# The experts as straight-line code: three groups of 256 tokens for the first, one of 128 for each other, and a general path behind one branch

## The chip, the cores and the metric

The kernel runs on one core of a Trainium2 chip. The metric is the device time of one execution, in microseconds. A run of it is compared with runs of the kernel before on the same chip, and medians are compared.

## The reference

Three layers follow each other. An attention with a decaying state, 4 batches of 768 tokens, 8 heads of 48 features; a feed-forward layer with softplus over all 3072 tokens; and a layer of eight experts that each token enters with its best expert alone, or not at all.

```python
def _attn_ref(q, k, v, f_logit):
    f = 1.0 / (1.0 + np.exp(-f_logit))
    for t in range(S):
        state = f[:, :, t, :, None] * state + np.einsum('bhd,bhe->bhde', k[:, :, t], v[:, :, t])
        y[:, :, t] = np.einsum('bhd,bhde->bhe', q[:, :, t], state)

def _moe_ref(x, w_in, w_out):            # [3072, 384] @ [384, 2048], [2048, 384]
    h = x @ w_in
    g = np.maximum(h, 0.0) + np.log1p(np.exp(-np.abs(h)))
    return g @ w_out

def _moe2_ref(x, w_skip, w_gate, w1, w2): # w1: 8 x [384, 1024], w2: 8 x [1024, 384]
    do_compute = x @ w_skip > 0
    xc = x[do_compute]
    logits = xc @ w_gate
    e_idx = np.argmax(logits, axis=1)
    gate_w = softmax(logits)[np.arange(len(xc)), e_idx]
    for e in range(8):
        mask = e_idx == e
        h = np.maximum(xc[mask] @ w1[e], 0.0)
        y[mask] = gate_w[mask, None] * (h @ w2[e])
    out = x.copy(); out[do_compute] = xc + y
```

How many tokens an expert gets depends on the data, so the kernel learns it while it runs.

## The kernel before

Every product that must be exact is made of three matmuls: each operand is split in a rounded part (`hi`, a 32-bit type that TensorE takes in one pass) and what that lacks (`lo`), and hi x hi, hi x lo and lo x hi are added up. Plain float32 is used where little is computed.

The program runs in 96 steps, eight for each unit of 256 tokens. A step has one eighth of the unit's feed-forward layer: `Ffn.up` (L417: 18 matmuls of 256 columns into `ph`), the softplus on ScalarE, VectorE and GpSimd (L432 to L453), and `Ffn.down` two steps later (L464: 12 matmuls of 394 columns into `acc`). The last columns of `w_out` carry its product with the routing weights, so the routing logits come out with the features. The attention of later tokens (L238 to L387) and the conversion of the weights lie between these steps. `Route` then picks each token's expert, stores the token's row to `x_s` in memory, and writes its number into a table sorted by expert. The last unit's numbers go by a shorter way (`last_route`: `place`, L537, and `set_ids`, L604).

The experts take turns, the one with most tokens first. An expert's weights come in quarters (`w_load`, L641; halves of w1, then of w2), are split by `w_split` (L656: the `hi` cast on ScalarE L665, the `lo` difference L673, on VectorE or GpSimd), and live in slots that are given out and back in the order of the program. A tile of 128 tokens is gathered by its numbers (L681), turned by three transposes (`turn`, L691), and taken through `expert` (L929): `up` (L941) with the tokens as weights and w1 as the moving operand in pieces of 512, 256 and 256 columns, a relu, eight transposes (`flip`, L947) that turn the hidden layer, `down` (L958) with 384 columns, the result `om` (L987) and the scatter of its rows to the output (L988).

The first expert's first tile is prepared beside the layer (`first_ids`). Before the experts one branch asks two flags (L901), and each expert's further tiles stand under branches of their own (`more`, L992, on the count that is loaded into a register). What stands inside a branch is scheduled by itself. Outside, a scheduler orders the instructions of each engine; `pin` keeps those of the experts in the order written. Each engine takes its instructions in that order, and SyncE (SP) issues the loads and stores in its own.

Of the kernel before, what the change touches and what calls it, by code (L numbers as in the profile page):

```python
# [19 lines left out]
P = 128  # L20
UNIT = 256
NEST = 6
FIRST = 0
FILL = (4, 2, 2, 5)
FILL0 = (0, 0, 2, 5)
AHEAD = 4
# [16 lines left out]
def gla_softplus_moe_kernel(  # L43
# [22 lines left out]
    E, _, F2 = w1.shape  # L66
# [15 lines left out]
    mw = ctx.enter_context(tc.tile_pool(name="mw", bufs=1))  # L82
    ps = ctx.enter_context(tc.tile_pool(name="ps", bufs=1, space=PSUM))
    main = ctx.enter_context(ExitStack())
    first = ctx.enter_context(ExitStack())
    att = first.enter_context(tc.tile_pool(name="att", bufs=2, side="right"))
    ffn = main.enter_context(tc.tile_pool(name="ffn", bufs=2))
    wp = main.enter_context(tc.tile_pool(name="wp", bufs=1))

    def psm(name):  # L90
        return ps.tile([P, 512], F32, tag="m", name=name, bufs=4)

# [26 lines left out]
    id0 = const.tile([P, 2], I32, name="id0")  # L119
# [12 lines left out]
    wo_hi = wp.tile([P, NF, XR], F32R, name="wo_hi")  # L132
    wo_lo = wp.tile([P, NF, XR], F32R, name="wo_lo")
# [3 lines left out]
    def setup():  # L137
# [7 lines left out]
        # [s <= t]  # L145
# [16 lines left out]
        ve.memset(hmax, 0.0)  # L162
        for t in [a_all, ut] + v_end:
# [25 lines left out]
    def conv_w(g, j):  # L189
# [3 lines left out]
        sl = (slice(None), slice(None), slice(g * n, (g + 1) * n)) if j == 0 else \  # L193
            (slice(None), slice(2 * g, 2 * g + 2), slice(0, DM))
        hw, lw = (wi_hi[sl], wi_lo[sl]) if j == 0 else (wo_hi[sl], wo_lo[sl])
# [3 lines left out]
        # below the least float32 the value is taken as 0  # L199
# [11 lines left out]
    def route_cols(g, w):  # L211
        """w_out @ [w_skip | w_gate] for two tiles of its rows, so that a token's logits come with its features."""
# [12 lines left out]
        if g % 2:  # L225
# [4 lines left out]
            sl = (slice(None), slice(2 * g - 2, 2 * g + 2), slice(DM, XR))  # L230
            se.copy(wo_hi[sl], src)
            ve.tensor_tensor(wo_lo[sl], src, wo_hi[sl].bitcast(F32), op=ALU.subtract)  # L232

# [15 lines left out]
    def a_pre(c):  # L249
# [4 lines left out]
        # the decay's exponent since the chunk's first token, then from its middle  # L254
# [8 lines left out]
        # a decay beyond the bound is taken step by step  # L263
# [16 lines left out]
    def split_qk(qt, kt):  # L280
        """Both in two exact parts, with q's heads side by side and zeros on the other head's rows."""
# [31 lines left out]
    def a_score(c):  # L313
# [14 lines left out]
        # the heads of a pair sit on different rows of the array: a PSUM bank each  # L328
# [25 lines left out]
        # 32 of the array's columns each: the first features of four heads, or the last of a pair  # L354
# [46 lines left out]
    class Ffn:  # L401
# [7 lines left out]
        def up(self, i):  # L409
            xh, xl = self.x  # L410
            ph = ps.tile([P, 2, UNIT], F32, tag="h", name=f"ph{i}", bufs=2)
            for j in range(2):
                f0 = (2 * i + j) * P
                n = 0
                for kk in range(KD):
                    for w, x in ((wi_hi, xh), (wi_hi, xl), (wi_lo, xh)):
                        te.matmul(ph[:, j, :], lhsT=w[:, kk, f0:f0 + P], rhs=x[:, kk, :],  # L417
# [220 lines left out]
    def w_free(kind, n):  # L638
        slots.append(taken.pop((kind, n)))
# [231 lines left out]
    def redo_unit(b, j):  # L871
# [19 lines left out]
        if final:  # L891
            return
# [218 lines left out]
```

## Time and profile before

| | us |
|---|---|
| median of three runs | 897.87 |
| the runs | 898.48, 897.87, 888.36 |
| span of the profiled execution | 890.6 |
| TensorE busy | 735.6 |
| VectorE busy | 690.5 |
| last matmul of the feed-forward layer ends | 687.05 |
| last matmul of the experts ends | 879.76 |

The profiled execution's time is known by its span, from the first to the last instruction; what lies around it is not shown. TensorE's matmuls overlap, so what one costs in a series is the distance between two starts, and not its duration. The granted clock is the mean share of full speed that TensorE got in a stretch; it has two levels, 1.2 and 2.4 GHz.

### The profile page before, as it was taken

The page shows a single profiled execution, that of the slowest core. Times are in us where ns is not written, and L with a number is a line of the kernel's source. Part 1 is how long each engine was busy: PE and PEld are TensorE (multiplying, and loading weights), DVE is VectorE, ACT ScalarE, POOL GpSimd, SP SyncE. Part 2 cuts the span into 40 slices and gives each one's busy share as a digit, 9 for nine tenths or more (in the row PEclk, how much of TensorE's full clock was granted, in tenths as well). Part 3 has the DMA queues.
Part 4 walks back from the last instruction along what each step waited for, and adds up shares of the span by engine and source line. Part 5 has one row for each costly group of instructions (what it writes and reads, how often), then busy time and mean ns, then how long its engine had stood idle before and what let it go on. Part 6 is the DMA issues. An engine that isn't in the chain of part 4 may idle for free. (4 is left out here: it accounts for less than half of the span.)

```text
span 890.6 us, 15792 instructions
## 1 busy us (share of the span) xinstructions
PE 735.6 (83%) x5857; PEld 674.5 (76%) x5857; DVE 690.5 (78%) x1180; ACT 458.7 (52%) x881; POOL 464.9 (52%) x382
## 2 busy tenths in 40 slices
PE   1676788989989997998989799897997889777665
PEld 1465667979989886998878699897896789666554
DVE  7999998888798779788887978888786733756651
ACT  4555544556556555555556655554654422545430
POOL 7777766763665757375666635454442421334220
PEclk9989869999999999899999899999999899878877
DMA  9553221221111211112121110101511681555400
GB/s 297 162 157 111 82 66 40 77 32 56 42 58 44 63 48 51 47 42 76 42 72 35 50 55 23 47 1 41 210 37 30 214 270 36 169 167 177 158 22 5
DMA packets 44040, 75.97 MB, mean 85 GB/s; under 512 B 5439, under 2 KB 23186, under 8 KB 43920
## 3 DMA queue, kind: packets, MB, share of 16 engines
q1 hardware_dynamic: 41040, 68.66, 24.8%
q0 software_dynamic: 2880, 5.82, 2.2%
q8 instruction: 62, 1.02, 0.5%
q14 instruction: 58, 0.48, 0.2%
HBM read 63.23 MB, written 12.11 MB: 85 GB/s over the span
## 5 line engine op out<-in xcount | busy, mean ns | idle before, releaser
L444 POOL TENSOR_TENSOR w<-w,u 128x512 f32<-128x512 f32 x95 | 129.9, 1368 | 173.9 <-DVE u L437 133.8
L417 PE MATMUL ph<-xh,wi_hi 128*128 128x256 f32 x576 | 169.4, 294 | 22.9 <-DVE u L437 12.1
L417 PE MATMUL ph<-xl,wi_hi 128*128 128x256 f32 x576 | 165.5, 287 | 0.0
L417 PE MATMUL ph<-xh,wi_lo 128*128 128x256 f32 x576 | 164.8, 286 | 0.0
L464 PE MATMUL acc<-wo_hi,gh 128*128 128x394 f32 x384 | 139.0, 363 | 12.1 <-ACT gh L452 10.1
L464 PE MATMUL acc<-wo_hi,gl 128*128 128x394 f32 x384 | 132.7, 360 | 19.5 <-DVE gl L453 19.5
L464 PE MATMUL acc<-wo_lo,gh 128*128 128x394 f32 x384 | 134.6, 351 | 2.2 <-DVE wo_lo L232 2.2
L417 PEld LDWEIGHTS ph<-xh,wi_hi 128*128 128x128 f32 x576 | 113.0, 196 | 28.6 <-issue 11.0
L443 ACT ACTIVATE w<-w 128x512 f32<-128x512 f32 (+1 forms) x97 | 60.7, 626 | 104.6 <-DVE u L436 104.6
L417 PEld LDWEIGHTS ph<-xl,wi_hi 128*128 128x128 f32 x576 | 112.9, 196 | 0.3 <-issue 0.2
L417 PEld LDWEIGHTS ph<-xh,wi_lo 128*128 128x128 f32 x576 | 112.7, 196 | 0.2 <-issue 0.2
L434 DVE TENSOR_SCALAR w<-u 128x512 f32<-128x512 f32 (+1 forms) x97 | 71.7, 739 | 41.3 <-ACT u L433 39.7
L673 DVE TENSOR_TENSOR lo<-raw,hi 128x384 fp32r<-128x384 f32 (+1 forms) x88 | 65.1, 786 | 38.3 <-ACT hi L665 38.2
L464 PEld LDWEIGHTS acc<-wo_hi,gl 128*128 128x128 f32 x384 | 75.0, 196 | 25.4 <-DVE gl L453 24.8
L436 DVE SCALAR_TENSOR_TENSOR u<-w,u 128x512 f32<-128x512 f32 (+1 forms) x97 | 86.7, 894 | 1.7
L464 PEld LDWEIGHTS acc<-wo_hi,gh 128*128 128x128 f32 x384 | 74.3, 194 | 17.5 <-ACT gh L452 13.1
L452 ACT CAST gh<-w 128x512 fp32r<-128x512 f32 (+1 forms) x97 | 59.3, 611 | 47.0 <-POOL w L444 45.8
L453 DVE TENSOR_TENSOR gl<-w,gh 128x512 fp32r<-128x512 f32 (+1 forms) x89 | 65.7, 738 | 20.2 <-ACT gh L452 19.7
L464 PEld LDWEIGHTS acc<-wo_lo,gh 128*128 128x128 f32 x384 | 75.1, 196 | 2.8 <-DVE wo_lo L232 2.6
L432 ACT ACTIVATE u<-ph 128x512 f32<-128x512 f32 (+1 forms) x97 | 56.5, 582 | 23.0 <-PE ph L417 22.8
L437 DVE SCALAR_TENSOR_TENSOR u<-ph,u 128x512 f32<-128x512 f32 (+1 forms) x97 | 65.8, 679 | 2.3
L433 ACT ACTIVATE u<-u 128x512 f32<-128x512 f32 (+1 forms) x97 | 60.9, 628 | 1.3
(211 smaller groups left out, 1740.9 us busy)
## 6 DMA issues: line engine op xcount, KB each, us to landing
raw<-in_moe_w_dram SPq DMA_DIRECT2D x32, 768.0 KB
si<-in_moe_w_in_dram SPq DMA_DIRECT2D x8, 768.0 KB
so<-in_moe_w_out_dram SPq DMA_DIRECT2D x8, 768.0 KB
f<-in_f_logit_dram SPq DMA_DIRECT2D x24, 224.0 KB
q<-in_q_dram SPq DMA_DIRECT2D x24, 224.0 KB
k<-in_k_dram SPq DMA_DIRECT2D x24, 224.0 KB
x_s<-xr SPq DMA_DIRECT2D x24, 192.5 KB
v<-in_v_dram SPq DMA_DIRECT2D x24, 192.0 KB
```

The lines of the kernel that those rows point to most:

```text
L417: te.matmul(ph[:, j, :], lhsT=w[:, kk, f0:f0 + P], rhs=x[:, kk, :], start=(n == 0), stop=(n == 3 * KD - 1))
L432: se.activation(u[:, c], ph[:, c], AF.Abs)
L433: se.activation(u[:, c], u[:, c], AF.Exp, scale=-1.0)
L434: ve.tensor_scalar(w[:, c], u[:, c], 1.0, None, op0=ALU.add)
L436: ve.scalar_tensor_tensor(u[:, c], w[:, c], 1.0, u[:, c], op0=ALU.subtract, op1=ALU.subtract)
L437: ve.scalar_tensor_tensor(u[:, c], ph[:, c], 0.0, u[:, c], op0=ALU.max, op1=ALU.subtract)
L443: se.activation(w[:, c], w[:, c], AF.Ln)
L444: (ve if i in self.fine else ge).tensor_tensor(w[:, c], w[:, c], u[:, c], op=ALU.add)
L452: se.copy(flat(gh)[:, c], w[:, c])
L453: (ge if i < self.pool_steps else ve).tensor_tensor(flat(gl)[:, c], w[:, c], flat(gh)[:, c].bitcast(F32), op=ALU.subtract)
L464: te.matmul(self.acc[t][:, 0:XR], lhsT=g[:, j, t * P:(t + 1) * P], rhs=w[:, f, :], start=(f == 0 and n == 0), stop=(f == NF - 1 and n == 2))
L673: pin((ge if i == 0 and n % 4 != 1 else ve).tensor_tensor(lo[:, i], t[:, i], hi[:, i].bitcast(F32), op=ALU.subtract))
```

## The change

The experts become one straight line of code without branches. The first expert gets `UNITS0` = 3 groups of 256 tokens, each other expert one tile of 128, whatever the counts are. Two flags (a decay that is too strong; now also any expert over its places, `flag_counts`) are asked once, at the end: where one is set, a general path does the experts again. It is in the program but not part of the main line.

A group or tile is a `Tiles`. Its `up` has w1 as the weights and the tokens as the moving operand, 256 columns wide for a group and 128 for a tile, so the hidden layer comes out with its features on the partitions, and the transposes of `flip` are gone. `act` makes both parts straight from PSUM. A step of `down` follows the next step's `up`. The splits are two pieces of 768 a quarter, ScalarE then VectorE (GpSimd has none); `feed` puts up to three of them behind each step of a tile, and issues loads when slots are free. The layer's weights are tiles per step, so that memory for the experts' weights comes free step by step. On the host w1 and w2 are laid out so that a quarter is one run of 6 KB per partition. The layer's own matmuls and activations stay.

```diff
-NEST = 6
-FIRST = 0
-FILL = (4, 2, 2, 5)
-FILL0 = (0, 0, 2, 5)
-AHEAD = 4
+UNITS0 = 3
+TILES0 = UNITS0 * UNIT // P
+PIECES = 2
+FILL = (0, 0, 2, 3) + (3,) * 64
...
-    wi_hi = wp.tile([P, KD, DFF], F32R, name="wi_hi")
-    wi_lo = wp.tile([P, KD, DFF], F32R, name="wi_lo")
...
+        for g in range(STEPS):
+            wi_hi[g] = wp.tile([P, KD, 2 * P], F32R, name=f"wi_hi{g}")
+            wi_lo[g] = wp.tile([P, KD, 2 * P], F32R, name=f"wi_lo{g}")
...
+    def w_piece(n, i):
+        m = KD * F2 // 2 // PIECES
+        t, hi, lo = (w.rearrange("p a c -> p (a c)")[:, i * m:(i + 1) * m] for w in (raw[n], w_hi[n], w_lo[n]))
+        pin(se.copy(hi, t))
+        pin(ve.tensor_tensor(lo, t, hi.bitcast(F32), op=ALU.subtract))
+        if i == PIECES - 1:
+            slots.append(taken[n].pop(0))
+    def feed(n):
+        while True:
+            while wanted and len(slots) >= (1 if wanted[0][0] == "load" else 2):
+                what, q = wanted.pop(0)
+                if what == "load":
+                    w_load(q)
+                else:
+                    pieces.extend(w_split(q))
+            if n <= 0 or not pieces:
+                return
+            w_piece(*pieces.pop(0))
+            n -= 1
+    class Tiles:
...
+        def up(self, i):
+            xh, xl = self.x
+            ph = self.ph[i] = ps.tile([P, self.per, self.n * P], F32, tag="h", name=f"phm{i}", bufs=2)
+            for j in range(self.per):
+                f = i * self.per + j
+                g, c = 4 * self.e + f // 4, slice(f % 4 * P, (f % 4 + 1) * P)
+                n = 0
+                for kk in range(KD):
+                    for w, x in ((w_hi[g], xh), (w_hi[g], xl), (w_lo[g], xh)):
+                        pin(te.matmul(ph[:, j, :], lhsT=w[:, kk, c], rhs=x[:, kk, :], start=(n == 0),
+                                      stop=(n == 3 * KD - 1)))
+                        n += 1
+        def act(self, i):
+            ph = self.ph.pop(i).rearrange("p a b -> p (a b)")
+            gh, gl = (pools["mo"].tile([P, self.per, self.n * P], F32R, tag=nm, name=nm) for nm in ("hh", "hl"))
+            flat = lambda a: a.rearrange("p a b -> p (a b)")
+            pin(se.activation(flat(gh), ph, AF.Relu))
+            pin(ve.scalar_tensor_tensor(flat(gl), ph, 0.0, flat(gh).bitcast(F32), op0=ALU.max, op1=ALU.subtract))
...
-    bad, redo = flags()
-    with tc.If(redo > 0, preferred_fallthrough_block=False):
...
+    wanted += [("load", n) for n in range(4, 12)] + [("split", n) for n in range(4, 8)] + [("load", n) for n in range(12, 16)]
+    for e in range(2, E):
+        wanted += [("split", n) for n in range(4 * e, 4 * e + 4)]
+        if e + 2 < E:
+            wanted += [("load", n) for n in range(4 * e + 8, 4 * e + 12)]
+    feed(0)
+    pinned.append(True)
+    route = last_route()
+    next(route)
...
+    for at in range(len(seq) + 1):
+        if at < len(seq):
+            w, i = seq[at]
+            while pieces and pieces[0][0] <= 4 * w.e + (1 if i == 0 else 3):
+                w_piece(*pieces.pop(0))
+            w.up(i)
+            w.act(i)
...
+        feed(FILL[at])
+        if at >= 1:
+            w, i = seq[at - 1]
+            w.down(i)
...
+    some = nc.values_load(flag[0:1, 1:2], min_val=0, max_val=1)
...
+    with tc.If(some > 0, preferred_fallthrough_block=False), ExitStack() as gen:
```

Three places where instructions stand otherwise than before. First TensorE at the end of the feed-forward layer (`acc` are the layer's sums, `phm` the experts' hidden layer, `first` the first tokens), before:

```order
L464 MATMUL acc_7405<-wo_hi,gl 128x394
L568 MATMUL pids<-ident,rows 128x96
L903 UNCONDITIONAL_BRANCH x2
L523 MATMUL pr<-roh,before 128x16
L524 MATMUL pr<-cnt_last,ones 128x16
L554 MATMUL pplace<-pcol,prow 128x192
L608 MATMUL pcnt<-cnt_all,ones 128x8
L554 MATMUL pplace<-pcol,prow 128x192
L691 MATMUL pxg<-ident,xg_7573 128x128 x3
L902 UNCONDITIONAL_BRANCH
L941 MATMUL phm_11991<-hi_7246,first_7749 128x512
```

and now:

```order
L736 MATMUL phm_7858<-first_7581,w_7270 128x256
L736 MATMUL phm_7858<-first_7581,w_7269 128x256
L736 MATMUL phm_7858<-first_7582,w_7269 128x256
L481 MATMUL acc_7422<-wo_hi_130,gh 128x394
L481 MATMUL acc_7422<-wo_lo_131,gh 128x394
L481 MATMUL acc_7423<-wo_hi_130,gh 128x394
L481 MATMUL acc_7423<-wo_lo_131,gh 128x394
L736 MATMUL phm_7858<-first_7581,w_7270 128x256
```

The experts' matmuls, behind a branch before (whose rows between are not run unless a flag is set), now stand between the layer's last ones. The first 18 of them, the first group's first step of `up`, come ahead of the routing of the last unit.

Second SyncE's queue, around the last unit's stores (`out_dram` and `x_s`). Now, in this order, nine loads stand ahead of these stores, eight of them like the last one shown:

```order
L666 DMA w_7789<-in_moe_w_dram 128x1536
L666 DMA w_7803<-in_moe_w_dram 128x1536
L666 DMA w_7813<-in_moe_w_dram 128x1536
L502 DMA out_dram<-xr 128x384 x2
L528 DMA x_s<-xr 128x385 x2
L666 DMA w_8002<-in_moe_w_dram 128x1536
```

Before, two loads stood there and the other 26 behind the branch. All but the first of the nine now wait for TensorE to have done with a piece of the layer's weights.

Third VectorE, through one expert of one tile (`w` are weights in split, `hl` the lower part of the hidden layer, `xl` that of the next tile's turned tokens, `om` the result):

```order
L745 SCALAR_TENSOR_TENSOR hl<-phm_9102,hh 128x512
L677 TENSOR_TENSOR w_9010<-w_8847,w_9009 128x768 x2
L677 TENSOR_TENSOR w_9074<-w_8849,w_9073 128x768 x2
L745 SCALAR_TENSOR_TENSOR hl<-phm_9174,hh 128x512
L677 TENSOR_TENSOR w_9144<-w_8851,w_9143 128x768 x2
L677 TENSOR_TENSOR w_9146<-w_8853,w_9145 128x768
L764 SCALAR_TENSOR_TENSOR om<-pom,xg 128x384
L411 TENSOR_TENSOR xl<-pxg,xh 128x384
L677 TENSOR_TENSOR w_9146<-w_8853,w_9145 128x768
```

All eight pieces of the next expert's weights lie on VectorE now, four and four around the tile's own two evacuations, in place of 11 of 14 smaller ones, the other three on GpSimd.

## Rows read from the trace of the kernel before

**Rows 1.** The page: the span, and busy time of each engine, share, count.

```profile
span 890.6 us, 15792 instructions
...
PE 735.6 (83%) x5857; PEld 674.5 (76%) x5857; DVE 690.5 (78%) x1180; ACT 458.7 (52%) x881; POOL 464.9 (52%) x382
```

**Rows 2.** Busy time of each engine by stretch, then granted clock, DMA share, GB/s.

```profile
0.00:20.00 20.00, 2.28 (x16) 2.04 (x18) 16.46 (x30) 8.88 (x13) 14.19 (x29) 1.00 0.94 293
...
640.00:660.00 20.00, 19.79 (x128) 19.27 (x127) 16.42 (x35) 10.29 (x19) 8.10 (x7) 0.91 0.29 105
...
740.00:760.00 20.00, 19.57 (x126) 18.18 (x125) 6.97 (x15) 6.10 (x13) 4.66 (x5) 1.00 0.14 41
...
820.00:840.00 20.00, 11.77 (x60) 9.80 (x59) 11.87 (x18) 8.19 (x19) 5.62 (x6) 0.83 0.55 178
```

**Rows 3.** Timeline of L987, the tiles' results: start, us, instruction, wait before it.

```profile
758.54 0.62 DVE L987 SCALAR_TENSOR_TENSOR om<-pom,xg 128x384 f32<-128x384 f32 x1 [0.69 <-PE pom L958]
773.01 0.61 DVE L987 SCALAR_TENSOR_TENSOR om<-pom,xg 128x384 f32<-128x384 f32 x1
...
879.80 0.62 DVE L987 SCALAR_TENSOR_TENSOR om<-pom,xg 128x384 f32<-128x384 f32 x1 [1.06 <-PE pom L958]
```

**Rows 4.** Timeline of TensorE: the layer's end, the experts' start and end.

```profile
686.53 0.52 PE L464 MATMUL acc<-wo_hi,gl 128*128 128x394 f32 x2
690.99 0.76 PE L941 MATMUL phm<-hi,first 128*128 128x512 f32 x1 [3.94 <-DVE rmx L512]
...
879.42 0.34 PE L958 MATMUL pom<-hi,hl 128*128 128x384 f32 x1
```

**Rows 5.** Waits from 765 to 880 us: who, for whom, us, times, longest.

```profile
PE phm L941 <- issue: 27.6, 6, 5.7
```

**Rows 6.** Timeline of TensorE: series at full clock, first and last starts.

```profile
153.20 0.84 PE L224 MATMUL pw<-wt,wsg 128*32 128x128 f32 x6
...
300.63 0.28 PE L417 MATMUL ph<-xh,wi_hi 128*128 128x256 f32 x1
...
301.91 0.28 PE L417 MATMUL ph<-xh,wi_lo 128*128 128x256 f32 x1
...
762.18 0.60 PE L947 MATMUL pht<-ident,hr 128*128 128x128 f32 x4
...
875.75 0.33 PE L958 MATMUL pom<-lo,hh 128*128 128x384 f32 x1
...
877.31 0.34 PE L958 MATMUL pom<-lo,hh 128*128 128x384 f32 x1
```

**Rows 7.** Single lines, durations in ns (min/median/max); last: a group, us and mean.

```profile
L365 PEld LDWEIGHTS py<-a_sb,v x14: 107/110/112, 302.1 to 302.6; 128*32 128x32 f32 x14
L365 PE MATMUL py<-a_sb,v x14: 270/273/298, 302.1 to 302.7; 128*32 128x128 f32 x14
...
L376 PEld LDWEIGHTS pu<-v,kn x62: 119/123/126, 206.6 to 279.1; 128*48 128x48 f32 x62
...
L417 PEld LDWEIGHTS ph<-xh,wi_hi 128*128 128x128 f32 x576 | 113.0, 196 | 28.6 <-issue 11.0
```

**Rows 8.** Timelines of GpSimd (first gather by the full numbers) and SyncE (weight loads).

```profile
701.45 1.02 POOL L681 DMA_INDIRECT xg<-x_s,idg  x1 [1.88 <-DVE tp L612]
...
704.57 126.13 SPq L648 DMA_DIRECT2D raw<-in_moe_w_dram  x24
```

**Rows 9.** VectorE and ScalarE: one split in the timeline, then groups by shape.

```profile
831.85 0.68 DVE L673 TENSOR_TENSOR lo<-raw,hi 128x512 fp32r<-128x512 f32 x1
...
L204 ACT CAST wi_hi<-tw 128x768 fp32r<-128x768 f32 x8 | 6.7, 832 | 16.8 <-DVE tw L203 16.8
L951 DVE TENSOR_TENSOR hl<-pht,hh 128x512 fp32r<-128x512 f32 x13 | 9.0, 690 | 4.1 <-ACT hh L950 4.1
L987 DVE SCALAR_TENSOR_TENSOR om<-pom,xg 128x384 f32<-128x384 f32 x13 | 8.0, 612 | 4.5 <-PE pom L958 4.5
L393 DVE TENSOR_TENSOR xgl<-pxg,xgh 128x384 fp32r<-128x384 f32 x12 | 6.6, 550 | 2.9 <-ACT xgh L392 2.8
```

More of the change, by code (lines that the diff above doesn't have):

```diff
@@ L806, in last_route @@
         yield
+    flag = const.tile([1, 2], I32, name="flag")
     def flags():
@@ L822, in flags, with flag_counts @@
                                 op1=ALU.max)
-        return [nc.values_load(flag[0:1, i:i + 1], min_val=0, max_val=1) for i in range(2)]
+    def flag_counts():
+        t = last.pool.tile([P, E], F32, tag="tq", name="tq", bufs=1)
+        ve.tensor_tensor(t, cnt_all, caps, op=ALU.is_gt)
+        ve.tensor_reduce(over, t, axis=AX.X, op=ALU.max)
+        ve.tensor_tensor(flag[:, 1:2], flag[:, 1:2], over[0:1, :], op=ALU.max)
     def scan_head(b, p, j):
@@ L879, in redo_unit @@
         f = Ffn(xs)
-        final = isinstance(b, int) and (b + 1) * S == NT and (j + 1) * UNIT == S
-        f.acc = last.acc if final else [psm(f"acr{t}") for t in range(CPU)]
+        f.acc = [psm(f"acr{t}") for t in range(CPU)]
         for i in range(STEPS):
@@ L899, in redo_unit @@
             r.scatter(t)
-    bad, redo = flags()
-    with tc.If(redo > 0, preferred_fallthrough_block=False):
-        with tc.If(bad > 0):
+    flags()
+    main.close()
+    mo = pools["mo"] = rest.enter_context(tc.tile_pool(name="mo", bufs=2, reuse_waits="tile"))
+    slots += [("mo", f"w{i}") for i in range(16)]
+    wanted += [("load", n) for n in range(4, 12)] + [("split", n) for n in range(4, 8)] + [("load", n) for n in range(12, 16)]
[3 more added lines that the diff above has]
+            wanted += [("load", n) for n in range(4 * e + 8, 4 * e + 12)]
@@ new lines, in gla_softplus_moe_kernel @@
+    pinned.clear()
+    some = nc.values_load(flag[0:1, 1:2], min_val=0, max_val=1)
+    rest.close()
+    general = ctx.enter_context(ExitStack())
+    ffn = general.enter_context(tc.tile_pool(name="gffn", bufs=2))
+    with tc.If(some > 0, preferred_fallthrough_block=False), ExitStack() as gen:
+        bad = nc.values_load(flag[0:1, 0:1], min_val=0, max_val=1)
+        with tc.If(bad > 0), ExitStack() as again:
+            mw, att, wp = (again.enter_context(tc.tile_pool(name=f"g{nm}", bufs=1)) for nm in ("mw", "att", "wp"))
+            wsg = att.tile([P, KD, 32], F32, name="gwsg")
+            ve.memset(wsg, 0.0)
+            load_wsg()
+            ffn_weights()
+            for g in range(STEPS):
+                load_w(g)
+                for j in range(2):
+                    conv_w(g, j)
@@ L1063 @@
+                    w = Tiles(e, [c[:, 1:2]], ("acc0",), [mo.tile([P, KD, P], F32R, tag=f"gx{i}", name="gx") for i in range(2)])
+                    w.fetch([c[:, 0:1]], "mo")
+                    w.turn()
+                    for i in range(w.steps):
+                        w.up(i)
+                        w.act(i)
+                        w.down(i)
+                    w.out()
 _INS = ["q", "k", "v", "f_logit", "moe_w_in", "moe_w_out", "moe2_w_skip", "moe2_w_gate", "moe2_w1", "moe2_w2"]
```

378 lines of the change are left out of this document (155 added, 223 removed).

## The prediction

> **What bounds the kernel now.** I read the page's busy times first [rows 1]. TensorE is the busiest engine with 735.6 us of a span of 890.6, but that is a mean over stages, so the next view is the busy time by stretch [rows 2]. Beside the feed-forward layer (640 to 660 us) TensorE is busy 19.79 of 20 us: nothing but fewer matmuls would shorten that stage, and the change leaves its matmuls alone. In a stretch of the late experts (820 to 840) it is busy 11.77 of 20 us at a mean granted clock of 0.83: part of the time it ran at the lower of its two levels (1.2 and 2.4 GHz). The change is about this stage.
>
> The timeline of the line that finishes a tile of the experts dates them [rows 3]. There are 13 such rows. The sixth tile ends at 758.54 and the seventh at 773.01, and after it six more come by 879.80, (879.80 - 773.01) / 6 = 17.8 us each. So the first expert took six tiles (641 to 768 tokens) and each other expert one (at most 128). From the last matmul of the feed-forward layer to the first of the experts TensorE idles 3.94 us [rows 4]: from the end of that last matmul (687.05) to that of the last of the experts (879.76) the stage takes 192.7 us. The waits between 765 and 880 us say what the late experts wait for: TensorE stood 27.6 us in six waits with "issue" as the releaser, which no semaphore explains [rows 5]. They stand where one expert's code ends and the next one's begins, around the branches of `more`. That is 27.6 / 6 = 4.6 us of each 17.8.
>
> **The change, part by part.**
>
> *The path taken.* Three groups of 256 hold 768 tokens and seven tiles 128 each. Rows 3 say that this input fits. The other condition of the flag, 256 tokens of the first expert before the last unit, also holds: at least 641, less at most the 256 of that unit, leaves 385. The general path is skipped.
>
> *Branches and flags.* Seven conditional pieces go, and with them the 4.6 us per expert. The one left comes after the last tile, where the kernel before has one too: from the last matmul's end (879.76) to the end of the span lie 10.8 us [rows 4], and I keep them.
>
> *TensorE's work.* All prices are intervals between starts at full clock [rows 6]. A 256-column matmul of the same type: 300.63 to 301.91 over 11 steps, 0.116 us. A 384-column one: 875.75 to 877.31 over 9 steps, 0.173 us. A transpose: four in 0.60, 0.15 us.
> - A group of 256 tokens: 72 matmuls of 256 columns up, 8.35 us, and 48 of 384 columns down, 8.30 us; 16.65, three times: 50.0 us. The 8 transposes of the hidden layer per tile are gone, because w1 is now the weight and the hidden layer comes out as it is needed.
> - One of the other experts: 72 matmuls of 128 columns up and 24 of 384 down (4.15 us). No row has this type at 128 columns. From below it is bounded by its columns, half of 0.116: 0.058 us. From above by plain float32, whose 128-column matmul appears as two records: six in 0.84 us, and one lasts 0.273 [rows 7], so starts are (0.84 - 0.273) / 5 = 0.113 apart, which makes 0.226 us a matmul. Between them lies the weight load. Loads take 0.110 us for 32 columns, 0.123 for 48 and 0.196 for 128 [rows 7], 0.90 ns a column, so 128 columns occupy 0.115 us, and a new one is needed for each matmul. That is nearest to the 256-column row, so I take 0.116: half the columns at no gain. 72 x 0.116 + 4.15 = 12.5 us, seven times: 87.5 us.
> - The Trainium skill (TensorE: Matmul & The Clock Gate, section on LDWEIGHTS) speaks against this part as well: a load takes columns / 1.2 GHz, 107 ns for 128 columns, whatever the matmul behind it. By that rule the 504 matmuls would take 54 us and not 58.5, and the forecast would be 850; the slope of rows 7 agrees with it to a tenth.
> - Turning gathered rows: 33 transposes, 5.0 us.
> - The first group's first 18 matmuls (2.1 us) now stand between the last ones of the layer, where TensorE waits for its activations and then the 3.94 us: hidden.
>
> Sum: 50.0 + 87.5 + 5.0 - 2.1 = 140.4 us.
>
> *New waits.* (a) The second group needs the token numbers with the last unit in them. They were ready at 701.45, when GpSimd began its gathers [rows 8], 14.4 us after the layer; the rest of the first group fills 16.65 - 2.1 = 14.5 us, then two gathers of 1.02 us each must be issued and land. I take 3 us; 0 if the numbers come sooner now, 6 if not. (b) The last step of the last tile waits for ScalarE and VectorE, some 1.3 us. (c) Splits stand in program order with the tiles' own evacuations. A split that waits for its weights holds ScalarE and VectorE, behind it the evacuation of the running step, and behind that TensorE's `down`. I take 5 us over seven experts, between 0 and the price of rival 3. Together 9.3.
>
> *What is taken as free, and its cover.* Splitting: eight pieces of 768 per expert, all on VectorE now (GpSimd did some before). A 512-wide one takes 0.68 us alone [rows 9], so 768 some 1.02. With two evacuations of 0.69, one of 0.55 and one of 0.61 that is 10.7 us per expert, under TensorE's 12.5 + 0.45; ScalarE's eight casts are 8 x 0.832 = 6.7. This cover is 2.2 us thin: if TensorE gets faster, VectorE is the bound. Weights: the nine loads ahead of the last unit's stores on SyncE's queue wait for pieces of the layer's weights to come free, and the stores wait for the layer's last matmul anyway, as those loads do; they cost nothing and land beside the layer. 19 more quarters remain for 150 us. Before, 24 took 126.13 us from the first issue to the last [rows 8], 5.3 us each; at that rate 19 take 100. At the rate of the start (293 GB/s, rows 2) one takes 2.7.
>
> *The total.* 140.4 + 9.3 = 149.7 us in place of 192.7, so 43 less: a span of 848. The span before is 890.6, and the page gives no time around it; the runs' median is 897.87, 7.3 above, and the lowest, 888.36, is below it. I carry the 7.3 over: **855 us**.
>
> **Rivals.**
> 1. *128 columns are taken at float32's price* (slower than before). At 0.226 us the 504 matmuls cost 504 x 0.110 = 55 us more: 910 us, 1.4% over the median. It decides from 0.116 + 43 / 504 = 0.20 us a matmul on. For: nowhere does the kernel before give this type fewer than 256 columns; its attention pads q with zeros to reach 256. Against: every matmul of this type is one record in the trace and plain float32 two.
> 2. *128 columns cost what they are.* At 0.058 us TensorE needs 8.8 us per expert, and VectorE's 10.7 is the bound: 7 x (12.95 - 10.7) = 16 us less, 839. For: weight loads overlap matmuls, and rows 7 have a fixed part that they may share. Against: the slope of rows 7. The Trainium skill (same page, section on the back-to-back gap) has 81 ns for pairs of a load and a 128-column matmul, which would end here too, since VectorE would still be the bound; no run here shows it.
> 3. *The gaps stay in another form.* Splits arrive late, TensorE stands and its clock falls as in rows 2. At a clock of 0.83 the 7 x 12.95 = 91 us of the seven experts become 110, 19 more, and 2 us of standing per expert make 14 where (c) has 5: together 28 more, 883. For: each expert's weights go through load, ScalarE and VectorE just one expert ahead, and loads 16 to 31 can only be issued once the first expert's slots are free. Against: 5.3 us a quarter would suffice, and in 740 to 760, where the first expert's tiles follow each other without a break, the clock was 1.00.
> 4. *The general path runs after all*: 13 tiles again, each with its 12.5 us at least: over 1,000 us. Rows 3 speak against it.
>
> **Numbers.** Forecast 0.55; its own range is 847 (no waits (a) and (c)) to 872 (wait (a) at 6, 2 us per expert at (c), and 5 us for a layer that the scheduler ordered anew). Rival 2 has 0.13, rival 3 0.12, rival 1 0.15, rival 4 0.05. Rivals 1 and 4 make the 2 in 10 left out, so the range is 836 to 891: from rival 2 without wait (a) to rival 3 with wait (a) at 6 and those 5 us. A measurement tells 2% from no change, 18 us: under 880 is faster, over 916 slower. Forecast, rival 2 and a third of rival 3 give 0.72; the rest of rival 3 and most of rival 1 give 0.21 within; rival 4 and the upper end of rival 1 give 0.07.
>
> **What would show it.** In the profile after: no "issue" waits between experts; 13 results written by seven tiles and three pairs; TensorE's starts in the 128-column `up` 0.116 us apart (0.058 and 0.226 for rivals 2 and 1); finished late experts some 13 to 14 us apart in place of 17.8; a clock near 1.00 from 690 us on; no more than a few us of TensorE waiting for VectorE's or ScalarE's splits; weights landing before 687 us. It is wrong if the layer itself ends later than 687 by more than 5 us, since I take it as untouched, if the splits hold TensorE for more than 2 us per expert, or if the branch at the end costs more than the 10.8 us kept.

## The result, and the profile after

The changed kernel takes **871.02 us** in the median of 4 runs (868.43 to 871.37), the kernel before 897.61 of 4 (888.36 to 898.48): a ratio of 0.973, 95% interval 0.968 to 0.977. That is faster, by 26.6 us where the forecast had 43. In a second session the ratio was 0.969 (0.964 to 0.974).

The profiled execution took 871.06 us for a span of 869.4, so 1.7 us lie around a span. The page of the kernel after, as in [rows 1]:

```profile
span 869.4 us, 15749 instructions
...
PE 747.2 (86%) x6119; PEld 702.1 (81%) x6119; DVE 669.0 (77%) x1121; ACT 443.9 (51%) x806; POOL 423.1 (49%) x350
```

TensorE is busy 11.6 us longer and the span is 21.2 shorter: the change removed standing time and added matmul time. The stretches show where, in the columns of [rows 2] (span, then PE, PEld, DVE, ACT, POOL busy, granted clock, DMA share, GB/s):

```profile
680.00:700.00 20.00, 15.46 (x90) 14.68 (x89) 9.19 (x25) 7.07 (x16) 4.54 (x4) 0.83 0.80 326
...
760.00:780.00 20.00, 19.21 (x116) 19.14 (x116) 8.79 (x13) 6.04 (x9) 2.46 (x3) 0.74 0.33 108
780.00:800.00 20.00, 20.00 (x161) 19.93 (x161) 12.40 (x17) 9.11 (x14) 2.37 (x3) 1.00 0.50 189
```

From 780 us on TensorE hardly stands (20.00 of 20 us) and runs at its full 2.4 GHz. Two stretches do not look like that: 680 to 700, with TensorE at 15.46, a clock of 0.83 and 326 GB/s of transfers beside it, and 760 to 780, nearly full but at 0.74.

The results of the experts in the timeline of VectorE answer to [rows 3] ("x2" is a group's pair):

```profile
727.67 1.14 DVE L764 SCALAR_TENSOR_TENSOR om<-pom,xg 128x384 f32<-128x384 f32 x2
744.76 0.61 DVE L764 SCALAR_TENSOR_TENSOR om<-pom,xg 128x384 f32<-128x384 f32 x1
745.62 0.62 DVE L764 SCALAR_TENSOR_TENSOR om<-pom,xg 128x384 f32<-128x384 f32 x1 [0.24 <-PE pom L757]
771.97 1.14 DVE L764 SCALAR_TENSOR_TENSOR om<-pom,xg 128x384 f32<-128x384 f32 x2
786.28 0.61 DVE L764 SCALAR_TENSOR_TENSOR om<-pom,xg 128x384 f32<-128x384 f32 x1
798.85 0.61 DVE L764 SCALAR_TENSOR_TENSOR om<-pom,xg 128x384 f32<-128x384 f32 x1
...
850.61 0.61 DVE L764 SCALAR_TENSOR_TENSOR om<-pom,xg 128x384 f32<-128x384 f32 x1
856.99 0.62 DVE L764 SCALAR_TENSOR_TENSOR om<-pom,xg 128x384 f32<-128x384 f32 x1 [2.91 <-PE pom L757]
```

Thirteen results in three pairs and seven singles; the late experts come 12.5 to 13.1 us apart in place of 17.8. The third pair comes 27 us after the second, though a group has 16.65 us of matmuls.

TensorE's timeline at the first tokens, the layer's end, at the second group's tokens, in the middle of a late expert and at the last matmul answers to [rows 4, 6] (start, us, instruction, wait before it):

```profile
688.29 0.90 PE L724 MATMUL pxg<-ident,xg 128*128 128x128 f32 x3 [4.15 <-DMA xg<-x_s,id]
...
700.09 0.52 PE L481 MATMUL acc<-wo_hi,gl 128*128 128x394 f32 x2
702.63 0.39 PE L540 MATMUL pr<-roh,before 128*128 128x16 f32 x2 [2.02 <-DVE roh L530]
...
719.97 0.38 PE L736 MATMUL phm<-xh,w 128*128 128x256 f32 x1 [0.89 <-ACT xh L410]
721.40 0.38 PE L736 MATMUL phm<-xl,w 128*128 128x256 f32 x1 [1.05 <-DVE xl L411]
...
790.77 0.27 PE L736 MATMUL phm<-xl,w 128*128 128x128 f32 x1
...
794.57 0.28 PE L736 MATMUL phm<-xh,w 128*128 128x128 f32 x1
...
856.61 0.34 PE L757 MATMUL pom<-w,hl 128*128 128x384 f32 x1
```

The 128-column matmul starts every (794.57 - 790.77) / 34 = 0.112 us: the forecast's 0.116, and no rival's 0.058 or 0.226. The Trainium skill (TensorE: Matmul & The Clock Gate, section on LDWEIGHTS) has the columns divided by 1.2 GHz for such a load, an estimate of 107 ns, and that lies as near. But the layer ends at 700.6, not 687.05, and its transposes of the first tokens stood 4.15 us for a gather.

The issues of SyncE (SPq) and the gathers of GpSimd beside that answer to [rows 8]. The first row is the first store of the output, which dates the execution:

```profile
171.50 1.07 SPq L502 DMA_DIRECT2D out_dram<-xr  x2
...
678.13 22.83 SPq L666 DMA_DIRECT2D w<-in_moe_w_dram  x9
```

The same store in the kernel before:

```profile
165.87 1.05 SPq L485 DMA_DIRECT2D out_dram<-xr  x2
```

The gathers:

```profile
681.34 1.05 POOL L699 DMA_INDIRECT xg<-x_s,id  x1 [4.29 <-DVE id L641]
...
711.27 1.01 POOL L699 DMA_INDIRECT xg<-x_s,idg  x1 [25.07 <-DVE over L896]
```

The nine weight loads did not lie beside the layer: they stood behind the table's rows on SyncE's queue, and eight of them went out together from 678.13 to 682.8, three us before the gather of the first tokens. The ninth waited for the layer's end.

The ledger, forecast against trace, from these rows: the first unit's output is stored at 171.50 us where it was at 165.87 (+5.6); from there to the layer's end 529.1 us where it was 521.2 (+7.9); from there to the last matmul's end 156.3 where 149.7 were forecast (+6.6); the tail 12.45 for 10.8 (+1.6). Together 21.7, of the 21.8 between the spans 869.4 and 847.6. The experiments take them one by one.

### The profile page after: what moved, and what is told of

The parts are those of the page before. It is cut to its first block, busy times and chain, and to the rows that moved or that the text cites. A ratio compares the mean times of both kernels' runs of the same rounds, so it can differ in the third digit from the quotient of the medians.

```text
span 869.4 us, 15749 instructions
## 1 busy us (share of the span) xinstructions
PE 747.2 (86%) x6119; PEld 702.1 (81%) x6119; DVE 669.0 (77%) x1121; ACT 443.9 (51%) x806; POOL 423.1 (49%) x350
## 5 line engine op out<-in xcount | busy, mean ns | idle before, releaser
L434 PE MATMUL ph<-xh,wi_hi 128*128 128x256 f32 x576 | 172.4, 300 | 23.5 <-DVE u L454 13.6
L434 PE MATMUL ph<-xl,wi_hi 128*128 128x256 f32 x576 | 168.1, 292 | 0.0
L434 PE MATMUL ph<-xh,wi_lo 128*128 128x256 f32 x576 | 167.8, 291 | 0.0
L481 PE MATMUL acc<-wo_hi,gh 128*128 128x394 f32 x384 | 139.7, 365 | 10.4 <-ACT gh L469 8.6
L434 PEld LDWEIGHTS ph<-xh,wi_hi 128*128 128x128 f32 x576 | 115.6, 201 | 29.4 <-issue 12.8
L434 PEld LDWEIGHTS ph<-xl,wi_hi 128*128 128x128 f32 x576 | 115.5, 201 | 0.3 <-issue 0.2
L434 PEld LDWEIGHTS ph<-xh,wi_lo 128*128 128x128 f32 x576 | 115.3, 200 | 0.2 <-issue 0.2
L451 DVE TENSOR_SCALAR w<-u 128x512 f32<-128x512 f32 (+1 forms) x97 | 66.7, 688 | 42.9 <-ACT u L450 42.8
L481 PEld LDWEIGHTS acc<-wo_hi,gl 128*128 128x128 f32 x384 | 75.1, 196 | 20.5 <-DVE gl L470 19.3
L470 DVE TENSOR_TENSOR gl<-w,gh 128x512 fp32r<-128x512 f32 (+1 forms) x89 | 63.9, 718 | 23.3 <-ACT gh L469 22.9
L736 PE MATMUL phm<-xh,w 128*128 128x128 f32 (+1 forms) x384 | 71.4, 284 | 1.9 <-ACT xh L410 1.7
L745 DVE SCALAR_TENSOR_TENSOR hl<-phm,hh 128x512 fp32r<-128x512 f32 x26 | 18.0, 691 | 64.0 <-ACT hh L744 62.7
```

Of the source, the lines that this page charges most:

```text
L434: te.matmul(ph[:, j, :], lhsT=w[i][:, kk, j * P:(j + 1) * P], rhs=x[:, kk, :], start=(n == 0), stop=(n == 3 * KD - 1))
L451: ve.tensor_scalar(w[:, c], u[:, c], 1.0, None, op0=ALU.add)
L470: (ge if i < self.pool_steps else ve).tensor_tensor(flat(gl)[:, c], w[:, c], flat(gh)[:, c].bitcast(F32), op=ALU.subtract)
L481: te.matmul(self.acc[t][:, 0:XR], lhsT=g[:, j, t * P:(t + 1) * P], rhs=w[f // 4][:, f % 4, :], start=(f == 0 and n == 0), stop=(f == NF - ...
L736: pin(te.matmul(ph[:, j, :], lhsT=w[:, kk, c], rhs=x[:, kk, :], start=(n == 0), stop=(n == 3 * KD - 1)))
L745: pin(ve.scalar_tensor_tensor(flat(gl), ph, 0.0, flat(gh).bitcast(F32), op0=ALU.max, op1=ALU.subtract))
```

## The experiments

The first four ran together on one chip, the next four on one, the last by itself, each time with runs of the kernel before (medians 896.57, 899.53 and 896.91 us).

**again.** No edit: the changed kernel and a second trace.

> The changed kernel once more, with a second trace. In the first trace the output rows of the first unit are stored at 171.50 us, in the kernel before at 165.87, though nothing of the change stands so early in the program. If the 5.6 us belong to the change (its order of loads or its pools), the store comes at about 171.5 again and the layer ends at about 700. If they belong to the one execution, the store can come anywhere between 165 and 172, the distance from it to the layer's end stays at 529, and the kernel's times spread by as much. The gather of the first tokens keeps TensorE waiting 4.5 us in either case, and 760 to 780 us shows a clock near 0.74 again if the half clock at the second expert is the program's.

870.81 us (865.48 to 872.34, 6 runs). The store came at 172.26. In nine traces of the changed kernel and of its variants below, whose programs are alike up to there, it came at 165.9, 166.1, 166.1, 167.7, 168.2, 169.8, 170.0, 171.5 and 172.3. So the 5.6 us belong to the execution and not to the change. The kernel before has them too: its profile has the store at 165.87, nobranch, the same program up to there, at 171.74. What decides it in the first 160 us stays open; the granted clock there differs from trace to trace. The distance to the layer's end was 529.2 again, and 760 to 780 us had a clock of 0.74 again. The half clock is the program's. The distance is so only in part: in the four other traces that keep the nine loads as they are it was 526.4 to 531.3.

**hold.** The first of the nine loads waits for the gather:

```diff
-        sy.dma_start(out=raw[n].rearrange("p a c -> p (a c)"), in_=src)
+        ins = sy.dma_start(out=raw[n].rearrange("p a c -> p (a c)"), in_=src)
+        if n == 4:
+            tc.add_manual_dep(ins.ins, firsts.got.ins.name,
+                              mybir.DependencyInfo(mybir.DependencyClass.Sync, mybir.DependencyReason.DATA))
```

`firsts.got` is the second of the two gathers.

> The first of the nine weight loads that are issued at 678 us waits until the first tokens' gather has landed; the others stand behind it. Theory, collision: the gather took 3.1 to 6.9 us to land because 326 GB/s of weight loads ran beside it. Then the wait of TensorE for the tokens (4.15 + 0.39 us) falls below 1 us, the half clock after it (688 to 693) goes, and the distance from the first unit's output store to the layer's end falls from 529 to about 522: 5 to 8 us less in all. Rival, the gather itself: two gathers issued 0.4 us later than the one before take that long anyway. Then the wait stays above 4 us, the distance at 529, and the loads land 5 us later: no change, or up to 5 us more.

866.22 us (861.74 to 868.60), 4.6 less than again and a little under the 5 to 8 expected, and the two ranges overlap; ratio to the kernel before 0.965 (0.961 to 0.970). The first gather, TensorE at the tokens and at the layer's end:

```profile
673.32 1.05 POOL L702 DMA_INDIRECT xg<-x_s,id  x1 [4.51 <-DVE id L641]
...
677.88 0.55 PE L727 MATMUL pxg<-ident,xg 128*128 128x128 f32 x3 [0.78 <-DMA xg<-x_s,id]
...
687.08 0.52 PE L481 MATMUL acc<-wo_hi,gl 128*128 128x394 f32 x2
```

The gathers, two of them as in the changed kernel, landed in 3.2 us (median) in place of 6.9, and TensorE stood 1.0 us for them in place of 4.5. The collision is shown, and the rival falls. Its price is read from the gather's issue to the layer's end: 14.3 us here and in both and flip, which hold the loads too, 19.3 in the changed kernel, 18.6 to 19.6 in all six traces without. That is 5.0 us. The distance from the store to the layer's end, 521.7 here, promises 7.4, but the other 2.4 lie ahead of the gather, where executions differ anyway (507.4 us from the store to the gather here, 507.4 to 512.0 in the nine traces).

And the stage behind the layer grew from 156.3 to 160.1: TensorE stood 2.4 us for the second group's tokens, a wait that the changed kernel doesn't have, and 740 to 760 us had a clock of 0.82. The gather of those tokens began 5.2 us after their numbers were ready:

```profile
697.18 0.26 DVE L630 TENSOR_SCALAR idg<-ids 128x192 int32<-128x192 int32 x1
...
702.59 1.01 POOL L702 DMA_INDIRECT xg<-x_s,idg  x1 [24.26 <-DVE w L680]
```

The trace's record of transfers says what it waited for: the last unit's rows (`x_s`), which it reads. Their stores were issued from 689.67 on, on the queue of the nine loads and behind them, and moved from 697.7 to 701.4, 1.2 us before the gather; in both they moved until 702.0, and the gather began at 703.24. So the held loads no longer meet the first gather, but they delay the second.

**turn.** The second expert's tokens are turned one step of TensorE earlier:

```diff
-if at < len(seq) and turned < len(work) and turned <= now + 1 and seq[at][1] == seq[at][0].steps - (2 if now >= UNITS0 else 1):
+if at < len(seq) and turned < len(work) and turned <= now + 1 and seq[at][1] == seq[at][0].steps - (2 if now >= UNITS0 - 1 else 1):
```

> The second expert's tokens are turned one step sooner (a step of 4.2 us of TensorE), between the third group's last two steps, so that their split is not asked for right behind the turn. Theory, gap: the waits of 0.83 and 1.03 us at 759 and 761 make the clock fall to half from 762 to 771, with 128-column matmuls 0.21 us apart in place of 0.112. Then both waits go, the clock of that stretch is 1.00, and 5 to 7 us are gained. Rival, the half clock has another cause (the stretch of 18.1 busy us in 740 to 760): the waits go, the clock stays near 0.74, and 2 us at most are gained.

864.64 us (856.44 to 865.75), 6.2 less than again; ratio 0.962 (0.957 to 0.967). First the changed kernel at that place, TensorE with the two engines that it waits for:

```profile
757.57 2.70 DVE L677 TENSOR_TENSOR w<-w,w 128x768 fp32r<-128x768 f32 x3
...
759.44 0.33 PE L736 MATMUL phm<-xh,w 128*128 128x128 f32 x1 [0.83 <-ACT xh L410]
760.79 0.33 PE L736 MATMUL phm<-xl,w 128*128 128x128 f32 x1 [1.03 <-DVE xl L411]
```

Three pieces of a split stand on VectorE ahead of the tokens' own split; TensorE asks for it at once and waits twice, and from 761.8 on its matmuls start 0.21 us apart. The stretch of 760 to 780 with the turn moved, then the layer's last matmuls and the experts' last one:

```profile
760.00:780.00 20.00, 20.00 (x161) 19.93 (x161) 13.06 (x18) 9.13 (x14) 3.46 (x3) 1.00 0.47 152
```

```profile
700.59 0.52 PE L481 MATMUL acc<-wo_hi,gl 128*128 128x394 f32 x2
...
850.01 0.34 PE L757 MATMUL pom<-w,hl 128*128 128x384 f32 x1
```

Both waits are gone, and so is the half clock. The stage takes 149.2 us, 7.1 less, where the forecast had 149.7: this gap, with the clock that fell behind it, was the excess. The length of the waits alone doesn't say whether the clock falls: the second group's tokens wait for the same reason in the changed kernel (0.89 and 1.05 us, at 719.97 and 721.40), and the granted clock of 720 to 740 us is 1.00. What makes the difference no run shows.

**half.** Up projection of the first three late experts with 64 tokens, of the last four with 64 of each 128 hidden units.

```diff
-                        pin(te.matmul(ph[:, j, :], lhsT=w[:, kk, c], rhs=x[:, kk, :], start=(n == 0),
+                        pin(te.matmul(ph[0:self.nf, j, :], lhsT=w[:, kk, c], rhs=x[:, kk, 0:self.n * self.nt], start=(n == 0),
```

`nt` is 64 for the first three, `nf` (and the width of `c`) 64 for the last four; both are 128 elsewhere.

> In the up projection of the second to fourth expert in the order of work, only 64 of 128 tokens are multiplied; in that of the last four all tokens, but only 64 of 128 hidden units of each block (the rest of the computation is left out). Theory, the weights' load: 128 columns of 32-bit weights set the 0.112 us from start to start. Then the first three stay at 0.112, and the last four fall by about 64 columns at 0.90 ns, to 0.05 to 0.07. Rival, the moving columns: the first three fall to 0.056, the last four stay at 0.112. Second rival, a fixed price of an instruction: both stay at 0.112. Where matmuls get faster, VectorE's 10.7 us an expert is the next bound, so the outputs of the last four would come 10.5 to 11 us apart in place of 12.5 to 13.1 by the theory.

TensorE's timeline, first and last start of a series of 36 of either kind, at full clock:

```profile
805.18 0.28 PE L738 MATMUL phm<-xh,w 128*128 128x64 f32 x1
...
809.09 0.28 PE L738 MATMUL phm<-xh,w 128*128 128x64 f32 x1
...
815.85 0.30 PE L738 MATMUL phm<-xh,w 128*64 128x128 f32 x1
...
818.04 0.22 PE L738 MATMUL phm<-xh,w 128*64 128x128 f32 x1
```

Half the tokens: (809.09 - 805.18) / 35 = 0.112 us, nothing gained. Half the weights' columns: 0.063 us. So the load of the weights is the price of this matmul, and its moving columns are free up to 128. Of the last four experts' results the first three came 10.2 us apart, a little under the expected 10.5 to 11. The run's one time, 866.82 us, says little, since the clock stayed low from 760 to 803.

**both.** hold and turn in one kernel.

> The held loads and the sooner turn together. If the two losses are separate, their gains add: hold came out 4.6 us below the changed kernel (866.2 against 870.8) and turn 6.2 us (864.6), so about 860 (858 to 862). If one half clock only takes the other's place (in hold, 740 to 760 us had a clock of 0.82), no more than the better of the two: 863 to 865.

861.08 us (854.66 to 867.84), ratio 0.958 (0.951 to 0.964): near the sum, and the rival's 863 lies inside the spread. The trace has both cures: 522.4 us from store to layer's end, and a clock of 1.00 from 720 to 840.

**flip.** both, and the up projection of the late experts with the tokens as weights; the down products come a step later:

```diff
+            for kk in range(KD):
+                for x, w in ((xh, w_hi[g]), (xh, w_lo[g]), (xl, w_hi[g])):
+                    pin(te.matmul(ph, lhsT=x[:, kk, :], rhs=w[:, kk, :],
...
+            pin(se.activation(self.hr[i], ph, AF.Relu))
...
+            for j in range(self.per):
+                pin(te.transpose(pt[:, j * P:(j + 1) * P], hr[:, j * P:(j + 1) * P], ident))
...
+            pin(se.copy(flat(gh), pt))
+            pin(ve.tensor_tensor(flat(gl), pt, flat(gh).bitcast(F32), op=ALU.subtract))
...
+        feed(FILL[at] + (at < len(seq) and flip(seq[at][0])))
```

The last line gives four pieces of a split to each step of a late expert in place of three, which spreads its eight evenly; the gathered rows have six buffers in place of eight.

> Both, and for the seven late experts the up projection with the 128 tokens as weights and w1's 512 columns moving: 18 matmuls in place of 72, then ReLU, eight transposes of 128 columns back, and the split; the down products come one step later. Theory, the weights' load set the price of the up projection: 512 moving columns at the 0.18 us of 394 columns take 0.23, so 18 x 0.23 + 11 transposes x 0.15 + 24 x 0.173 = 10.0 us of TensorE in place of 12.6, and VectorE's 8 x 0.954 + 2 x 0.69 + 0.56 + 0.61 = 10.2 bounds: outputs 10.2 to 10.8 us apart, 7 x 2.2 = 15 us less than both, so 842 to 848. Rival, the longer chain (ReLU, transposes, split, each on another engine) makes TensorE wait in every step: 11.5 to 12.6 apart, 853 to 862.

**838.93 us** (835.72 to 843.09), ratio 0.934 (0.929 to 0.940): the fastest here, 22.1 us below both and below the 842 to 848 expected; the stage behind the layer takes 130.9 us, both's 152.0. The late experts' results, and a stretch of theirs:

```profile
783.45 0.61 DVE L789 SCALAR_TENSOR_TENSOR om<-pom,xg 128x384 f32<-128x384 f32 x1
...
812.19 0.61 DVE L789 SCALAR_TENSOR_TENSOR om<-pom,xg 128x384 f32<-128x384 f32 x1
818.59 0.62 DVE L789 SCALAR_TENSOR_TENSOR om<-pom,xg 128x384 f32<-128x384 f32 x1 [0.67 <-PE pom L782]
```

```profile
780.00:800.00 20.00, 20.00 (x112) 18.12 (x111) 19.52 (x25) 17.65 (x28) 2.00 (x2) 1.00 0.74 278
```

Three distances of 9.58 us each, with TensorE, VectorE and ScalarE all close to full. The two before them were 11.8 and 11.7; in the mean from the third group to the fifth late expert it is 10.4, within the 10.2 to 10.8 expected of VectorE's bound. The last distance, 6.40, is not an expert's price: the fifth result stood 2.9 us on VectorE behind the splits, the sixth came right behind its last matmul, and the last matmuls of the two end 9.2 us apart. TensorE never waits in this stretch, so the longer chain costs nothing there. What the even feeding of the splits adds to the turned operand was not separated.

**small.** The first expert's second and third group as four tiles of 128, the turn a step earlier from the second tile on:

```diff
-    for u in range(1, UNITS0):
-        work.append(Tiles(0, [ids[:, 0, 2 * u + t:2 * u + t + 1] for t in range(2)], ("acc0", "acc1"),
-                          firsts.x if u == 2 else two(2)))
+    for t in range(2, TILES0):
+        work.append(Tiles(0, [ids[:, 0, t:t + 1]], (f"acc{t % 2}",), two(1)))
```

> The changed kernel, with the first expert's second and third group as four tiles of 128 in place of two groups of 256. If a tile of 128 costs what the late experts cost (12.6 us) and a group 16.65, the kernel takes 4 x 12.6 - 2 x 16.65 = 17 us longer, 886 to 891, so that two groups carry more than half of the change's 27 us. If other waits bound that stretch (the routing's numbers, the weights' splits), less than 10 us: 872 to 880.

875.12 us (872.16 to 880.90); its ratio of 0.976 (0.969 to 0.984) can't be told from again's 0.969 (0.964 to 0.974). The trace says why it is so little:

```profile
735.48 0.62 DVE L764 SCALAR_TENSOR_TENSOR om<-pom,xg 128x384 f32<-128x384 f32 x1 [0.85 <-PE pom L757]
748.07 0.62 DVE L764 SCALAR_TENSOR_TENSOR om<-pom,xg 128x384 f32<-128x384 f32 x1 [0.85 <-PE pom L757]
```

The tiles cost 12.6 us each, as expected, and with the turn's place changed the clock does not fall at the second expert (760 to 780 us: 1.00). Its stage of 165.7 us is 9.4 over the changed kernel's 156.3, and 16.5 over turn's 149.2, which like it has no half clock there: that is the expected 17. The 17 were right and the verdict of 872 to 880 came out all the same, because this kernel also undoes a loss that it was not meant to touch.

**notail.** No general path and no branch to it.

```diff
-    some = nc.values_load(flag[0:1, 1:2], min_val=0, max_val=1)
-    with tc.If(some > 0, preferred_fallthrough_block=False), ExitStack() as gen:
...
```

> The changed kernel without the general path at its end and without the branch to it (left out: what is done for inputs that need it; these do not). The changed kernel's trace ends 12.45 us after the last matmul. If the branch is on the path that sets the end, as its engines meet for it after the last store is issued, 2 to 6 us of them go. If the last store's landing and the program's end set it, 11 to 12.5 stay.

One run, 865.86 us, with a span of 864.1 us. The last matmul in its timeline:

```profile
857.02 0.34 PE L757 MATMUL pom<-w,hl 128*128 128x384 f32 x1
```

From the last matmul's end to the span's 6.7 us in place of 12.45: the branch that is never taken costs 5.7 us, with the load of its flag, on the path that sets the end.

**nobranch.** The kernel before, without the late experts' branches:

```diff
-        more(e, n, second, *((xt2, xg["third"]) if e == 0 else ()))
+        if e == 0:
+            more(e, n, second, xt2, xg["third"])
```

> The kernel before, without the seven late experts' branches to further tiles (line 1034 for e > 0, with the gather for a second tile and the count's load; the first expert keeps its own). Its late experts have at most 128 tokens here, so what is left out would not run. Its up projection already has the tokens as weights. Theory, branches: the 4.6 us of issue waits an expert go and the clock stays up, so TensorE's own work (18 x 0.231 + 11 x 0.15 + 24 x 0.18 = 10.1 us) and the splits bound it: outputs 10 to 13 us apart in place of 17.8, 30 to 50 us less than before: 848 to 868, below the changed kernel's 871. Then the turned up projection and the groups of 256 were not what made the change faster. Rival, the weights: 24 quarters took 126 us, 5.3 each, four an expert; the loads wait for each other in pairs, and the outputs stay 15 to 17 us apart: 880 to 892.

**855.69 us** (853.20 to 858.54), ratio 0.954 (0.950 to 0.959), and below the changed kernel's 871. It isn't general, but it prices the branches, with the second tile's gather and the count's load that go with them: 41 us. The layer's last matmuls, results of the first and the sixth late expert, and the last matmul, with a stretch:

```profile
693.87 0.52 PE L464 MATMUL acc<-wo_hi,gl 128*128 128x394 f32 x2
...
777.15 0.60 DVE L987 SCALAR_TENSOR_TENSOR om<-pom,xg 128x384 f32<-128x384 f32 x1
...
838.37 0.60 DVE L987 SCALAR_TENSOR_TENSOR om<-pom,xg 128x384 f32<-128x384 f32 x1
...
846.71 0.34 PE L958 MATMUL pom<-hi,hl 128*128 128x384 f32 x1
```

```profile
780.00:800.00 20.00, 15.72 (x97) 13.93 (x96) 19.59 (x27) 13.50 (x32) 11.42 (x10) 1.00 0.80 260
```

The stage behind the layer takes 152.7 us, 40 less than before, and the tail 6.85 in place of 10.8. The late experts come 11.1 to 13.7 us apart, 12.2 in the mean, bound by VectorE (19.59 of 20) and not by TensorE (15.72). The first expert's last tiles, whose weights are split already, come 9.66 apart: that was the matmul price of this form all along.

The first store came at 171.74, nearly as in the changed kernel's trace, so the two spans, 853.9 and 869.4, can be set side by side. Of the 15.5 us between them 6.5 lie ahead of the layer's end, the 5.0 of the nine loads among them, 5.6 in the tail, and 3.7 in the stage behind the layer, which is less than the 7.1 of the half clock.

## Why the prediction was right, and where it was not

- **The gaps at branches** go, and they carry the gain. Right, and larger than I had it: nobranch takes 40 us out of this stage, where I saw 4.6 us of issue waits in each late expert. How the rest divides between the clock that falls beside them [rows 2] and the work that can now run across the experts' borders was not separated.
- **0.116 us for a 128-column matmul.** Right (0.112), and for the reason given: half shows that the weights' load sets it. Rivals 1 and 2 fall, and the 81 ns that rival 2 quotes is not met here.
- **50.0 + 87.5 + 5.0 of TensorE.** Right as a sum: with the waits, turn's stage is 149.2 us where 149.7 were forecast. It is not right term by term. The waits of TensorE in it are 5.4 us, not 9.3. The 0.15 us of a transpose is a row of four divided by four [rows 6], and not a distance of starts: in the changed kernel three take 0.24 us from their start to the next matmul's (771.70 to 771.94), so 33 cost 2.6 us and not 5.0. On the other side the sum lacks the routing's matmuls and the slower ones behind them (a clock of 0.91 in 700 to 720 us). And the 2.1 us taken off as hidden fall into no wait: in the changed kernel TensorE works without a break from 690.57 to the layer's end. What the layer would take without them was not tried.
- **What the sum left unsaid.** I added up the new stage and took the old one as 192.7 in a lump. The trace of before had the old price of a tile in plain sight, two lines above the first of [rows 3] in the same timeline:

```profile
739.23 0.62 DVE L987 SCALAR_TENSOR_TENSOR om<-pom,xg 128x384 f32<-128x384 f32 x1 [0.68 <-PE pom L958]
748.88 0.62 DVE L987 SCALAR_TENSOR_TENSOR om<-pom,xg 128x384 f32<-128x384 f32 x1 [0.70 <-PE pom L958]
```

  9.65 us a tile in the first expert, against my 12.5 for the new form. That is the old form's price on TensorE alone, with no weights to split beside it. With the old splits beside it a late expert takes 12.2 (nobranch), about as much as the new form does; with the new splits it takes 9.6 at best and 10.4 in the mean (flip, which gains 22.1). So the new form, at 12.5 to 13.1, lost little against the kernel before, but it left 22 us lying. "The branches go, the splits get lighter, the new form of the tile costs" would have been the right split, and it names the better kernel.
- **"They cost nothing and land beside the layer"**, of the nine loads. This step failed. I looked at whom the loads hold up on SyncE's queue and not at when they would go: behind the table's rows, eight in one burst, against the first tokens' gather. From that gather's issue to the layer's end it takes 19.3 us with them and 14.3 with hold: 5.0 us. The rest of the ledger's 7.9 lies mostly ahead of the gather, where executions differ.
- **(c), splits in program order, 5 us, and a clock near 1.00 from 690 us on.** The mechanism is right, but not where I had it, and larger. From 780 us on TensorE hardly waits for a split. Ahead of that the tokens' own split stood behind three pieces of weights twice, 1.9 us of waiting each: at the second group, where the clock stayed up, and at the second expert's first matmul, where it fell: 7.1 us with what turn saves.
- **(a), 3 us for the second group's numbers.** They cost nothing here: the gathers by them began at 711.27, 10.7 us after the layer's end, and TensorE did not wait for them. The 1.9 us that it stood at that turn are the split of (c). What I had not is the 2.02 us for the last unit's routing at 702.63.
- **The tail kept at 10.8.** Short by 1.6; the branch in it costs 5.7 (notail), a price that the kernel before paid as well: nobranch, whose last expert has no branch behind it, ends 6.85 us after its last matmul.
- **7.3 us between the profiled span and the median.** Right as a step, though I had no reason for it: 1.7 lie around the span, and the profiled execution was an early one by its first store, which moves over 6.4 us.
- **Rival 3** (gaps in another form, clock 0.83) is what happened in part, in 680 to 700 and 760 to 780, and not in the experts' run where I had put it.
- **The signs of being wrong.** Two of the three came up: the layer ended 13.6 us after 687 (5.6 of them the execution's), and the tail took 12.45 us where 10.8 were kept. The sum had no term for either; the total stayed in the range because the range was wide.

Still open: how the launch decides the first 160 us, and why the clock falls behind one of two like waits.

## What to carry to other kernels

When a change does several things, price each against the same piece of work before, from its own rows, and not the new sum against the old total: here the kernel before without its late branches gains 41 us, more than the whole change with its 26.6, and the total hid that another 22 could be had. A load that "waits anyway" still has a moment at which it goes; look at what else is in flight then, and what stands behind it on its queue: held until the first gather had landed, the loads delayed the second. And where an operand is turned on the engine that runs out first, put at least one step of work between the turn and its first use: waits of 1.9 us cost 7.1 here, with the clock that fell behind them.

## What was not expected of the hardware

- A matmul of 32-bit weights, 128 columns of them, costs 0.112 us with 64 or with 128 moving columns, and [rows 6] has 0.116 for 256. Below 256 columns it is the load that is paid for.
- At the lower clock (1.2 GHz) the 128-token matmuls of the changed kernel start 0.21 us apart (from 761.8 on), and so do the 64-token ones of half, 0.213 us in a stretch whose granted clock is 0.50 (762.0 to 766.4). So at half the clock the load takes twice as long, and 64 moving columns still cost as much as 128:

```profile
760.69 0.61 PE L738 MATMUL phm<-xh,w 128*128 128x64 f32 x2
...
766.45 0.40 PE L738 MATMUL phm<-xh,w 128*128 128x64 f32 x1
```
- In nobranch VectorE's 512-wide split takes 1.225 us in the mean of 777 to 839 us, with GpSimd busy for 30.34 of these 62; in flip, where GpSimd does 5.02 of 41 (771 to 812), a 768-wide one takes 0.953. Three of nobranch's take 4.0 to 4.3 us, and each of the three spans a run of three splits on GpSimd, as here:

```profile
781.34 4.26 DVE L673 TENSOR_TENSOR lo<-raw,hi 128x512 fp32r<-128x512 f32 x1
```

```profile
781.83 3.21 POOL L673 TENSOR_TENSOR lo<-raw,hi 128x512 fp32r<-128x512 f32 x3
```

  VectorE's ended only behind all three. So it seems that a split on GpSimd holds up the one on VectorE; a kernel that differs in this alone was not run.
